# The output product of the last pair of tiles as seven half-size products, with operand sums on VectorE and weight sums made in slices ahead of it

## The chip, the core and the metric

The kernel runs on one core of one Trainium2 chip. The core has a matrix engine (TensorE: PE for its matmuls, PEld for its weight loads), VectorE (DVE), ScalarE (ACT), GpSimd (POOL) and SyncE (SP), which issues all of the kernel's transfers into one queue served by 16 DMA engines. The metric is the device time of one execution, in microseconds. Before the change the median of 3 runs is 935.18 us (934.85 to 935.95).

## What is computed

Attention in chunks of 64 tokens, and then a gated feed-forward layer with a root-mean-square norm, all in float32. There are 8 x 576 = 4608 tokens, 8 heads of 64, a model width of 512 and a hidden width of 1536.

```python
scores = scale * np.matmul(q_c, k_c.transpose(0, 1, 2, 4, 3))     # chunks of 64
scores = scores - np.max(scores, axis=-1, keepdims=True)
attn = np.exp(scores)
attn = attn / (np.sum(attn, axis=-1, keepdims=True) + 1e-09)
x = np.matmul(attn, v_c)                    # gathered to 4608 x 512
xn = x / np.sqrt(np.mean(x * x, axis=-1, keepdims=True) + 1e-06) * rms_g
g = xn @ w_gate                             # 512 x 1536
silu = g * (1.0 / (1.0 + np.exp(-g)))
out = (silu * (xn @ w_val)) @ w_out         # 1536 x 512
```

## The kernel before

**Tiles.** The 4608 tokens are nine tiles of 512. The first three ("plain", line 834) go one by one; the other six go as three pairs (line 909). A matmul takes 128 x 128 stationary and 128 x 512 moving values. Every float32 operand is split into a high part, rounded to the type that TensorE multiplies (F32R), and a low part, the rest; a product is three matmuls: high x high, high x low, low x high.

**A plain tile.** For each of 12 blocks f of 128 hidden columns, `gated` makes the gate and the value (24 matmuls), ACT and DVE make the gated result and its two parts, and `down` adds its share of the output to four PSUM banks (12 matmuls). During the first plain tile the weights are converted from 64-bit words; during the first two they are stored to DRAM in the form that the pairs read: `wsd` holds the operands of the up products, `wod` those of the output product (`wod[i]` for the f blocks 2i and 2i+1: both parts, 512 output columns).

**A pair, up.** For each of six f pairs i, `up_pair` (line 649) multiplies a 2 x 2 block matrix of weights by a 2 x 2 block matrix of two tiles of normed tokens with seven products instead of eight, named P1 to P7, in the order P1, P5, P6, P2, P3, P7, P4. One product is 12 matmuls (two outputs m, two halves of the contraction, three parts). It adds into a bank named a, b, c or d. After each one, `after` takes what it needs from PSUM: ACT copies or SiLU, DVE sums, POOL sums and the multiplications of gate by value. The results are `g`, six tiles, each of 2 f blocks x 2 token tiles x 512. The token operands `xp` are made by `x_sides` (line 590), with a scratch tile `t1` (one buffer); the weight operands are loaded by `ring_load` (line 626), three loads ahead (`AHEAD_R`).

**A pair, output.** For each of the two token tiles and each f pair, `split_g` (line 735) makes the two parts of g (ACT cast, DVE subtraction; two buffers of each), and `down` adds to four banks, 12 matmuls for each of 24 splits. The weights come from `wod` by `out_load`, three loads ahead, 1 MB each. At the end of a tile, four banks are copied out, alternately by DVE and ACT, and stored.

**Attention for the next pair.** While pairs one and two run, four units of 256 tokens each are made for the pair that follows. A unit is seven steps: load q, k and v; scores and softmax; a turn of the weights, written to DRAM (`away_e`); the turned weights read back (`eT`); the values (`ps_o`, matmuls); the same turn for its rows of x (`away_x`, back into `x` or `x2`). A counter is advanced once after each of the 42 up products and once in each of the 24 stretches of the output product; unit n has its seven steps at 4 + 10n + (-4, 0, 3, 5, 8, 11, 13). The third pair has no units.

**What sets the order.** From the second plain tile on PE's instructions run in the order in which the program writes them. The other engines' and SP's orders come from a planner that simulates the program with its own costs: an instruction is placed when its data and its buffer are there in that simulation, by its place in the program; those written inside `urgent()` count as 300 places earlier. Once placed, each queue keeps its order on the chip, and an instruction that has to wait holds those behind it.

## Time and profile before

| | us |
|---|---|
| median of 3 runs | 935.18 |
| range of the runs | 934.85 to 935.95 |
| the profiled execution | 936.39 |
| its span, first to last instruction | 934.6 |
| pair one, up products (368.0 to 492.5) | 124.5 |
| pair one, output product (492.5 to 559.6) | 67.1 |
| pair two, up products (559.6 to 684.1) | 124.5 |
| pair two, output product (684.1 to 751.2) | 67.1 |
| pair three, up products (751.19 to 865.43) | 114.24 |
| pair three, output product (865.43 to 930.72) | 65.29 |
| after the last matmul | 3.88 |

The stages before 368 us are the three plain tiles. The stage boundaries are read from the chain of waits, where PE goes from one product's name to the other. A row of a group gives the line, the engine, the operation, output<-inputs by the program's names, the count, then busy time and the mean duration in ns, then the idle time before it and what ended it. A row of the timeline begins with its start and its length in us. The granted clock of TensorE is 1.000 throughout.

### The profile page before, as it was taken

To read this page: it belongs to the slowest core of one execution; us is meant where nothing else is said; L and a number is where in the kernel's file an instruction comes from. 1 tells how busy PE (TensorE), PEld (TensorE's weight loads), DVE (VectorE), ACT (ScalarE), POOL (GpSimd) and SP (SyncE) were. 2 spreads that over 40 slices of the span, in tenths; PEclk is the share of its full clock that TensorE was granted. 3 is DMA by queue.
4 is the path that set the end of the run, shared out by engine and by line. 5 is a ranking of instruction groups with operands and counts; after the bars stand their busy time and mean duration, and the time that the engine had idled before them with its cause. 6 is when DMAs were issued, how large, how long until landed. Compare 5 with 4: busy or idle time off the path is not lost.

```text
span 934.6 us, 17360 instructions
## 1 busy us (share of the span) xinstructions
PE 905.9 (97%) x6936; PEld 742.2 (79%) x6936; DVE 516.2 (55%) x889; ACT 431.5 (46%) x697; POOL 172.7 (18%) x157
## 2 busy tenths in 40 slices
PE   4599999999999999999999999999999999999998
PEld 3478788888888788888888888888888888888886
DVE  5899983554546555754664735546656332333232
ACT  4999963453446543553444425445444223222222
POOL 0100012224200000233332002322330023224100
PEclk9999999999999999999999999999999999999999
DMA  8688998868975644767789666586987585337511
GB/s 338 248 310 309 329 367 318 264 236 250 308 275 150 187 148 154 270 218 280 253 288 348 269 269 256 213 289 188 335 311 265 239 329 211 135 135 296 243 46 46
DMA packets 78737, 231.84 MB, mean 248 GB/s; under 512 B 8384, under 2 KB 40128, under 8 KB 62912
## 3 DMA queue, kind: packets, MB, share of 16 engines
q1 hardware_dynamic: 78656, 230.72, 69.0%
q8 instruction: 55, 0.90, 0.4%
q14 instruction: 26, 0.21, 0.1%
HBM read 171.97 MB, written 58.72 MB: 247 GB/s over the span
## 4 chain that ended last, share of the span: by engine, by line
PE 85%; ACT 7%; DVE 4%; DMA 2%; issue 1%; SPq 1%; POOL 0%; ACTq 0%; DVEq 0%; POOLq 0%
PE acc L506 29%; PE ps_b L637 11%; PE ps_c L637 11%; PE ps_a L637 11%; PE ps_g L471 7%; PE ps_v L471 7%; PE ps_d L637 5%; PE ps_o L356 2%; PE ps_s L239 2%; ACT w L152 1%; ACT e L275 1%; ACT raw L153 1%; ACT parts L177 1%; DVE parts L185 1%; DMA x<-kT_dram 1%
## 5 line engine op out<-in xcount | busy, mean ns | idle before, releaser
L506 PE MATMUL acc<-wo,gh 128*128 128x512 f32 x576 | 177.6, 390 | 0.0
L506 PEld LDWEIGHTS acc<-wo,gh 128*128 128x128 f32 x576 | 108.0, 188 | 22.5
L506 PE MATMUL acc<-wo,gl 128*128 128x512 f32 x288 | 112.3, 390 | 0.0
L740 DVE TENSOR_TENSOR gl<-g,gh 128x512 fp32r<-128x512 f32 x72 | 49.7, 691 | 101.2 <-ACT gh L739 99.2
L637 PE MATMUL ps_b<-xp,wr 128*128 128x512 f32 x432 | 104.7, 391 | 0.0
L637 PE MATMUL ps_c<-xp,wr 128*128 128x512 f32 x432 | 104.3, 390 | 0.0
L637 PE MATMUL ps_a<-xp,wr 128*128 128x512 f32 x432 | 103.5, 390 | 0.0
L471 PE MATMUL ps_g<-xh,parts 128*128 128x512 f32 x288 | 97.1, 396 | 1.9 <-ACT sg L489 1.4
L739 ACT CAST gh<-g 128x512 fp32r<-128x512 f32 x72 | 44.8, 623 | 116.1 <-PE acc L506 110.9
L471 PE MATMUL ps_v<-xh,parts 128*128 128x512 f32 x288 | 95.7, 392 | 0.0
L637 PEld LDWEIGHTS ps_a<-xp,wr 128*128 128x128 f32 x432 | 80.9, 188 | 16.9
L637 PEld LDWEIGHTS ps_b<-xp,wr 128*128 128x128 f32 x432 | 80.6, 188 | 17.1
L637 PEld LDWEIGHTS ps_c<-xp,wr 128*128 128x128 f32 x432 | 80.8, 188 | 16.9
L506 PE MATMUL acc<-parts,gh 128*128 128x512 f32 x288 | 90.2, 394 | 0.0
L711 POOL TENSOR_TENSOR g<-u,u 128x512 f32<-128x512 f32 x18 | 23.2, 1289 | 342.1 <-DVE u L707 244.4
L423 POOL TENSOR_TENSOR ri<-ss,mhalf 128x1 f32<-128x1 f32 x36 | 23.7, 665 | 245.1 <-DVE ss L421 244.8
L471 PEld LDWEIGHTS ps_g<-xh,parts 128*128 128x128 f32 x288 | 54.3, 189 | 14.3 <-ACT sg L489 1.8
L471 PEld LDWEIGHTS ps_v<-xh,parts 128*128 128x128 f32 x288 | 54.5, 189 | 11.3
L506 PEld LDWEIGHTS acc<-wo,gl 128*128 128x128 f32 x288 | 54.1, 188 | 11.8 <-DVE gl L740 0.5
L506 PEld LDWEIGHTS acc<-parts,gh 128*128 128x128 f32 x288 | 53.3, 188 | 11.2
L506 PE MATMUL acc<-parts,gl 128*128 128x512 f32 x144 | 56.5, 392 | 0.0
L471 PE MATMUL ps_g<-xl,parts 128*128 128x512 f32 x144 | 56.4, 391 | 0.0
(105 smaller groups left out, 1393.2 us busy)
## 6 DMA issues: line engine op xcount, KB each, us to landing
wr<-wsd SPq DMA_DIRECT2D x63, 1024.0 KB, 7.8
wo<-wod SPq DMA_DIRECT2D x36, 1024.0 KB, 8.2
raw<-w_up_dram SPq DMA_DIRECT2D x12, 1024.0 KB, 9.4
vt<-v_dram SPq DMA_DIRECT2D x18, 512.0 KB, 6.7
wsd<-parts SPq DMA_DIRECT2D x18, 512.0 KB, 6.6
out_dram<-o SPq DMA_DIRECT2D x36, 256.0 KB, 2.2
qt<-qT_dram SPq DMA_DIRECT2D x17, 512.0 KB, 5.5
kt<-kT_dram SPq DMA_DIRECT2D x17, 512.0 KB, 5.9
```

The source lines that it names most:

```text
L152: nc.scalar.activation(w, high.bitcast(F32), AF.Abs, scale=2.0**16)
L153: nc.scalar.mul(low, low.bitcast(U32), 2.0**-29)
L177: nc.scalar.copy(parts[:, 0].rearrange("p i c -> p (i c)"), w)
L239: nc.tensor.matmul(st["s"][j][c * CH : (c + 1) * CH, pr], st["q"][rows, pr, tok : tok + CH], st["k"][rows, pr, tok : tok + CH], start=True ...
L356: nc.tensor.matmul(st["o"][(2 * c + t) * Q : (2 * c + t + 1) * Q, h * D : (h + 1) * D], eT[c][rows, t, h], vt[rows, c, h], start=True, sto ...
L423: nc.gpsimd.tensor_tensor(ri, ss, mhalf, op=ALU.pow)
L471: nc.tensor.matmul(ps, a[f][:, cols], b[dt], start=(dt == 0 and i == 0), stop=(dt == NDT - 1 and i == 2),)
L506: nc.tensor.matmul(acc[s], a[:, cols], b, start=(f == 0 and i == 0), stop=(f == NF - 1 and i == 2),)
L637: nc.tensor.matmul(ps, w[:, a, m, cols], xp[:, b, kt], start=start and kt == 0 and i == 0, stop=stop and kt == 1 and i == 2, skip_group_ch ...
L711: nc.gpsimd.tensor_tensor(g[:, 0, 1], kp["u2"], kept[0]["u2"], op=mult)
L739: nc.scalar.copy(gh, src)
L740: nc.vector.tensor_tensor(gl, src, gh.bitcast(F32), op=ALU.subtract)
```

## The change

In the last pair the output product is no longer two tiles one after the other. `last_down` treats it as a 2 x 2 block product: the stationary side is an f pair's weights (two f blocks by two halves of 256 output columns), the moving side the two f blocks by the two token tiles of g. It uses the same seven products and the same order as the up products, for each product all six f pairs, n = 0 to 41. One n is a split of one 128 x 512 operand and 6 matmuls (two blocks m of 128 output columns, three parts). The output comes out turned, 128 output columns by 512 tokens; it is stored so, and the host turns those 1024 rows.

- `last_sums` makes two differences of g's quarters after each up step i on DVE, into spare rows of `x` and `x2`, which no unit needs in the last pair. `split_next` updates the operand after its split in P5 and P2, on DVE.
- `split_g` gets a second pair of buffers in turn (those of the attention weights, `e` and `eT`), and the splits are asked for two ahead (`AHEAD_G`).
- `last_after` takes each product from PSUM and stores four quarters of 2 x 256 KB: after P2, P3, P7 and P4.
- The weights' sums are made in pairs one and two, by twelve slices of `out_sides`, six in each: steps 7n + 0 to 5 of the counter load a slice, copy three unsummed operands in DRAM, make five sums on DVE, round on ACT, subtract on DVE, store. The slice's tile has the tag of `t1` and its one buffer. `x_sides` takes `t1` at its first use instead of at its start. The result is a new DRAM tensor `wol`, read by `last_load`, four operands (1 MB) at a time.

```diff
+AHEAD_G = 2
+SIDE_STEPS = 0, 1, 2, 3, 4, 5
+NOS = (7 * NPR + 3) // 4
+INTO = {P1: "a", P2: "a", P6: "b", P7: "b", P5: "c", P3: "c", P4: "d"}
+FROM = {p: INTO[p] for p in (P1, P6, P5, P4)}
+LAST = P2, P7, P3, P4
...
+    wol_ = dram.tile([P, 7 * NPR, 2 * KH], F32, name="wol")
+    def out_sides(i, c):
+        at = {}
+        parts = wod[i].rearrange("p (a n c) -> p a n c", a=2, c=KH)[:, :, :, c * P : (c + 1) * P]
+        slots = wol_.rearrange("p (k i) c -> p i k c", i=NPR)[:, i, :, c * KH : (c + 1) * KH]
+        def load():
+            w = at["w"] = st.tile([P, 4, 2, P], F32, tag="t1", bufs=1, name="w")
+            for a in range(2):
+                nc.sync.dma_start(w[:, :, a], parts[:, a])
+        def plain():
+            for p, n in (P1, 0), (P2, 2), (P4, 3):
+                nc.sync.dma_start(slots[:, p].rearrange("p (a c) -> p a c", a=2), parts[:, :, n])
+        def sums():
+            w = at["w"]
+            nc.vector.tensor_tensor(w[:, :, 0], w[:, :, 0], w[:, :, 1], op=ALU.add)
+            a11, a21, a12, a22 = (w[:, n, 0] for n in range(4))
+            s1, s2, s4, s3 = (w[:, n, 1] for n in range(4))
+            for o, one, two, op in (
+                (s1, a21, a22, ALU.add),
+                (s2, s1, a11, ALU.subtract),
+                (s4, a12, s2, ALU.subtract),
+                (s3, a11, a21, ALU.subtract),
+            ):
+                nc.vector.tensor_tensor(o, one, two, op=op)
+        def high():
+            w = at["w"]
+            nc.scalar.copy(w[:, :, 0].bitcast(F32R), w[:, :, 1])
+        def low():
+            w = at["w"]
+            nc.vector.tensor_tensor(w[:, :, 1].bitcast(F32R), w[:, :, 1], w[:, :, 0], op=ALU.subtract)
+        def store():
+            w = at["w"].rearrange("p n a c -> p n (a c)")
+            nc.sync.dma_start(slots[:, P5 : P6 + 1], w[:, :2])
+            nc.sync.dma_start(slots[:, P3 : P7 + 1], w[:, 2:])
+        return [load, plain, sums, high, low, store]
...
-    def split_g(src):
-        gh = gp.tile([P, TT], F32R, name="gh")
-        gl = gp.tile([P, TT], F32R, name="gl")
+    def split_g(src, other=False):
+        pool, names = (att, ("e", "eT")) if other else (gp, ("gh", "gl"))
+        gh, gl = (pool.tile([P, TT], F32R, tag=n, name=n) for n in names)
...
+    def last_load(n):
+        k = min(4, 7 * NPR - 4 * n)
+        t = big([P, 4, 2, 2, P], F32R, "wo")
+        nc.sync.dma_start(
+            t[:, :k].rearrange("p n m a c -> p n (m a c)").bitcast(F32), wol_[:, 4 * n : 4 * n + k]
+        )
+        return t
+    def spare(i):
+        return (x, x2)[i // NSUB][:, i % NSUB]
+    def last_sums(i, g):
+        for o, one, two in (spare(i), g[:, 0, 1], g[:, 0, 0]), (g[:, 0, 1], g[:, 1, 1], g[:, 0, 1]):
+            nc.vector.tensor_tensor(o, one, two, op=ALU.subtract)
+    def last_down(t, gs, wos):
+        rows = out[t * TT : (t + 2) * TT, :].rearrange("(d a) c -> d (a c)", a=2)
+        split = {}
+        def split_next(n):
+            if n >= 7 * NPR:
+                return
+            p, i = divmod(n, NPR)
+            g, t1 = gs[i], spare(i)
+            src = {
+                P1: g[:, 0, 0], P5: t1, P6: t1, P2: g[:, 1, 0], P3: g[:, 1, 1], P7: g[:, 0, 1], P4: g[:, 1, 0]
+            }[p]
+            split[n] = split_g(src, n % 4 > 1)
+            with urgent():
+                if p == P5:
+                    nc.vector.tensor_tensor(t1, g[:, 1, 1], t1, op=ALU.subtract)
+                elif p == P2:
+                    nc.vector.tensor_tensor(g[:, 1, 0], t1, g[:, 1, 0], op=ALU.subtract)
...
+        for n in range(AHEAD_G):
+            split_next(n)
+        for n in range(7 * NPR):
+            p, i = divmod(n, NPR)
+            for k in range(n // 4, min(n // 4 + AHEAD_O, NOS)):
+                if k not in wos:
+                    wos[k] = last_load(k)
+            w = wos[n // 4][:, n % 4]
+            parts = split.pop(n)
+            for m in range(2):
+                if i == 0 and p in FROM:
+                    ps[m][FROM[p]] = bank(ps_h if p == P1 else ps_acc, f"ps_{FROM[p]}")
+                for k, (a, c) in enumerate(((0, 0), (0, 1), (1, 0))):
+                    nc.tensor.matmul(ps[m][INTO[p]], w[:, m, a], parts[c], ...)
+            split_next(n + AHEAD_G)
+            if i == NPR - 1:
+                with urgent():
+                    for m in range(2):
+                        last_after(p, m, ps[m], kept[m], store)
+    def last_after(p, m, b, kp, store):
+        # P1, P5: ACT copies; P6: one DVE sum; P2: ACT copy, store
+        # P3: one DVE sum, store; P7: two DVE sums, store
...
+        elif p == P4:
+            nc.vector.tensor_tensor(kp["p1"], kp["p1"], b["d"], op=ALU.subtract)
+            store(m, 1, 0, kp["p1"])
...
+        last_pair = b == NB - 1
+        if not last_pair:
+            for n in range(NPR):
+                for k, f in enumerate(out_sides(b * NPR // 2 + n // 2, n % 2)):
+                    at.setdefault(7 * n + SIDE_STEPS[k], []).append(f)
         for i in range(NPR):
-            gs.append(up_pair(i, step, wos))
+            gs.append(up_pair(i, step, wos, last_load if last_pair else out_load))
+            if last_pair:
+                last_sums(i, gs[i])
+        if last_pair:
+            last_down(t, gs, wos)
+            break
```

More of the change, by code (lines that the diff above doesn't have):

```diff
@@ L485, in gated @@
         sg = tmp_tile("sg")
-        gh = gp.tile([P, TT], F32R, name="gh")
-        gl = gp.tile([P, TT], F32R, name="gl")
+        gh = gp.tile([P, TT], F32R, tag="gh", name="gh")
+        gl = gp.tile([P, TT], F32R, tag="gl", name="gl")
         with urgent():
@@ L593, in x_sides, with t1 @@
         b11, b21, b12, b22 = x1[:, :, :2], x1[:, :, 2:], x2[:, :, :2], x2[:, :, 2:]
-        t1 = st.tile([P, 8, 2, 2 * Q], F32, tag="t1", bufs=1, name="t1")
         sub = ALU.subtract
+        later = {}
+        def t1():
+            if not later:
+                later[0] = st.tile([P, 8, 2, 2 * Q], F32, tag="t1", bufs=1, name="t1")
+            return later[0]
         def scale(x, dts):
@@ L611, in x_sides @@
             lambda: scale(x2, (0, 1)),
-            lambda: less(t1, b12, b11),
-            lambda: x_side(P5, t1),
+            lambda: less(t1(), b12, b11),
+            lambda: x_side(P5, t1()),
             lambda: scale(x2, (2, 3)),
-            lambda: less(t1, b22, t1),
-            lambda: x_side(P6, t1),
+            lambda: less(t1(), b22, t1()),
+            lambda: x_side(P6, t1()),
             lambda: x_side(P3, b22),
@@ L619, in x_sides @@
             lambda: x_side(P7, b12),
-            lambda: less(b21, t1, b21),
+            lambda: less(b21, t1(), b21),
             lambda: x_side(P4, b21),
@@ L647, in hold, with up_pair @@
         return xs.tile([P, TT], F32, tag="xs", name=name)
-    def up_pair(i, step, wos):
+    def up_pair(i, step, wos, wo_load):
         g = big([P, 2, 2, TT], F32, "g")
@@ new lines, in last_down, with store @@
+    def last_down(t, gs, wos):
[15 more added lines that the diff above has]
+                    nc.vector.tensor_tensor(g[:, 1, 0], t1, g[:, 1, 0], op=ALU.subtract)
+        def store(m, half, h, o):
+            at = half * KH + m * P
+            nc.sync.dma_start(rows[at : at + P, h * TT : (h + 1) * TT], o)
+        ps, kept = [{}, {}], [{}, {}]
+        for n in range(AHEAD_G):
[11 more added lines that the diff above has]
+                for k, (a, c) in enumerate(((0, 0), (0, 1), (1, 0))):
+                    nc.tensor.matmul(
+                        ps[m][INTO[p]],
+                        w[:, m, a],
+                        parts[c],
+                        start=p in FROM and i == 0 and k == 0,
+                        stop=p in LAST and i == NPR - 1 and k == 2,
+                        skip_group_check=True,
+                    )
+            split_next(n + AHEAD_G)
[3 more added lines that the diff above has]
+                        last_after(p, m, ps[m], kept[m], store)
@@ new lines, in last_after @@
+    def last_after(p, m, b, kp, store):
+        if p == P1:
+            kp["p1"] = hold("p1")
+            nc.scalar.copy(kp["p1"], b["a"])
+        elif p == P5:
+            kp["p5"] = hold("p5")
+            nc.scalar.copy(kp["p5"], b["c"])
+        elif p == P6:
+            kp["u2"] = hold("u2")
+            nc.vector.tensor_tensor(kp["u2"], b["b"], kp["p1"], op=ALU.add)
+        elif p == P2:
+            c11 = hold("c11")
+            nc.scalar.copy(c11, b["a"])
+            store(m, 0, 0, c11)
+        elif p == P3:
+            nc.vector.tensor_tensor(kp["u2"], b["c"], kp["u2"], op=ALU.add)
+            store(m, 0, 1, kp["u2"])
+        elif p == P7:
+            nc.vector.tensor_tensor(kp["p1"], b["b"], kp["p1"], op=ALU.add)
+            nc.vector.tensor_tensor(kp["p5"], kp["p1"], kp["p5"], op=ALU.add)
+            store(m, 1, 1, kp["p5"])
+        elif p == P4:
+            nc.vector.tensor_tensor(kp["p1"], kp["p1"], b["d"], op=ALU.subtract)
+            store(m, 1, 0, kp["p1"])
@@ L1003 @@
     rows = res.results[0]["out_dram"]
+    last = N - 2 * TT
+    rows = np.concatenate([rows[:last], rows[last:].reshape(DM, 2 * TT).T])
     turned = rows[2 * TT :].reshape(-1, 4, 2, Q, DM).transpose(0, 2, 1, 3, 4).reshape(-1, DM)
```

9 lines of the change are left out of this document (3 added, 6 removed).

## The prediction, made before the changed kernel was run

> **What bounds the kernel now.** I read the share of each engine first, then the busy time stage by stage, then the end of the chain of waits, and last the queues that feed it.
>
> ```profile
> PE 905.9 (97%) x6936; PEld 742.2 (79%) x6936; DVE 516.2 (55%) x889; ACT 431.5 (46%) x697; POOL 172.7 (18%) x157
> 276.70:368.00 91.30, 90.02 (x1054) 73.44 (x1053) 49.38 (x101) 44.81 (x65) 4.33 (x8) 1.00 0.52 154
> 368.00:492.50 124.50, 124.50 (x1146) 102.12 (x1145) 78.93 (x147) 61.55 (x93) 39.65 (x35) 1.00 0.75 263
> 559.60:684.10 124.50, 124.50 (x1146) 102.13 (x1145) 70.17 (x139) 57.97 (x89) 39.69 (x35) 1.00 0.73 257
> 751.19:865.43 114.24, 114.24 (x505) 94.63 (x505) 38.04 (x56) 30.55 (x51) 36.76 (x29) 1.00 0.60 228
> 865.43:930.72 65.29, 65.28 (x288) 53.73 (x287) 18.55 (x27) 15.48 (x26) 2.05 (x2) 1.00 0.25 100
> ```
>
> The five stretches are: most of the third plain tile; the up products of pairs one and two; the up products and the output product of the last pair. After the stretch and its length come the busy times of PE, PEld, DVE, ACT and POOL with their counts, the granted clock, the DMA share and GB/s. PE is full in each of the last four. So a matmul removed there is worth its spacing, and every stall newly put there is paid.
>
> ```profile
> 862.71 2.72 PE ps_d L637 x12
> 865.43 65.29 PE acc L506 x288
> 930.72 0.02 issue
> 930.75 0.58 ACT o L730
> ```
>
> The chain ends in the output product itself: 288 matmuls in 65.29 us, 226.7 ns each, without a break. An up product has the same spacing, 2.72/12 = 226.7 ns, with the weights as the stationary side, as they are in the new product. What follows the last matmul is one copy and its store.
>
> **Part 1, the output product.** It becomes 7 products x 6 pairs of f x 2 halves x 3 parts = 252 matmuls of the same shape. 36 fewer x 0.2267 = **8.16 us** less; the stage would take 57.13.
>
> [...]
>
> **Part 2, what feeds it.** A split now serves 6 matmuls, 1.36 us, where it served 12.
>
> ```profile
> L740 DVE TENSOR_TENSOR gl<-g,gh 128x512 fp32r<-128x512 f32 x22 | 15.2, 692 | 43.4 <-ACT gh L739 41.4 <-PE acc L506 2.0
> L739 ACT CAST gh<-g 128x512 fp32r<-128x512 f32 x22 | 13.7, 624 | 44.4 <-PE acc L506 44.4
> ```
>
> ACT has 0.62 us of work per 1.36, DVE 0.69; where P5 and P2 also update an operand, DVE has 1.38 per 1.36. Twelve such steps lose 12 x 0.02 = 0.2 us at worst and nothing if the splits run ahead. Four pairs of buffers let them: a split waits only for the product four before it. Today ACT waits for PE 44.4 us in this stage because two pairs are all it has. The evacuations add 10 DVE and 6 ACT operations in all, spread between products: DVE 42 + 12 + 10 = 64 x 0.69 = 44 of 57 us. Taken as 0; if splits did not overlap, see the third rival.
>
> The operand sums (12 DVE operations, 8.3 us) fall into the last pair's up stage, where DVE is busy 38 of 114 us. Only the sums of the last f pair come late:
>
> ```profile
> 864.89 1.30 POOL L705 TENSOR_TENSOR g<-p,p 128x512 f32<-128x512 f32 x1
> 866.37 1.29 POOL L717 TENSOR_TENSOR g<-p,p 128x512 f32<-128x512 f32 x1 [0.18 <-DVE p L713]
> 843.70 22.56 SPq L745 DMA_DIRECT2D wo<-wod  x12
> ```
>
> One waits on DVE for POOL until 866.2, with the next splits queued behind it; the first four splits have nothing to wait for and cover 5.4 us of PE. Uncovered it would be 866.2 + 0.7 - 865.4 = 1.5 us. Taken as 0. The weights come as 11 transfers instead of 12 and, as the last row shows, are issued before the stage begins: 0.
>
> **Part 3, the end.** The last operation is a DVE subtraction (0.69) where it was an ACT copy (0.58), then a store of the same 256 KB: **+0.11 us**.
>
> **Part 4, the slices.** Each of twelve slices is seven transfers (two loads of 256 KB, three copies of 128 KB from DRAM to DRAM, two stores of 256 KB), five DVE sums, one ACT cast and one DVE subtraction. The nearest rows:
>
> ```profile
> L305 DVE TENSOR_TENSOR e<-ps_s,mx 128x256 f32<-128x256 f32 x16 | 5.9, 412 | 0.0
> L574 DVE TENSOR_TENSOR w<-w,side 128x512 fp32r<-128x512 f32 x24 | 17.7, 771 | 17.1 <-ACT side L572 17.0
> L572 ACT CAST side<-w 128x512 fp32r<-128x512 f32 x24 | 13.6, 618 | 1.6 <-DVE gl L498 1.6
> q1 hardware_dynamic: 78656, 230.72, 69.0%
> w<-wfd SPq DMA_DIRECT2D x12, 512.0 KB, 5.4
> wsd<-w SPq DMA_DIRECT2D x24, 256.0 KB, 3.5
> ```
>
> DVE: 0.69 + 4 x 0.41 + 0.77 = 3.10 us a slice, 18.6 a pair: pair one's up stage goes from 78.9 to 97.5 of 124.5 us, pair two's to 88.8. ACT gains 3.7 a pair. Both fit. DMA: 1408 KB a slice, 17.3 MB in all; 230.72 MB takes 69.0% of the span, so this takes 5.2%, 48 us of all sixteen queues, into two stages that have 124.5 x (0.25 + 0.27) = 65 us free. It fits, narrowly. SP: 7 issues x 0.43 = 3.0 us a slice. A store waits on SP for DVE's subtraction, and the next load for that store (3.5 us, against two products, 5.44, between them); the ring loads queued behind are three ahead of PE, 3 x 5.44 = 16 us, and cover such waits.
>
> Where it can reach PE is the chain of the attention units, whose matmuls stand at fixed places in PE's order:
>
> ```profile
> 450.25 4.23 SPq L330 DMA_DIRECT2D away_e<-e  x2
> 454.54 0.42 SPq L629 DMA_DIRECT2D wr<-wsd  x1
> ...
> L339 SPq DMA_DIRECT2D eT<-away_e x8: 303/407/428, 455.1 to 460.0; - x8
> DMA to landing us min/median/max: 2.2/4.7/5.3
> 464.98 1.48 PE L356 MATMUL ps_o<-vt,eT 64*32 64x64 f32 x128
> PE ps_o L356 <- DMA eT<-away_e: 1.3, 2, 1.1
> ```
>
> In pair one's third unit the last read back is issued at 460.0 and lands 2.2 to 5.3 us later; PE uses it at 465.0. The margin is 2.8 us at best and none at worst. In the third plain tile (last row) PE already waited 1.3 us for such a read. A slice's load (512 KB, 5.4 us) written between a unit's write and its read back (the first and third units of a pair have one) holds SP and the queues ahead of the reads.
>
> The planner need not keep these places:
>
> ```profile
> 261.85 0.33 SPq L629 DMA_DIRECT2D wr<-wsd  x1
> 320.94 2.95 PE ps_g L471 x12
> ```
>
> A ring load written behind the product at 320.9 was issued at 261.8, because its buffer and data were there. The copies need no buffer, and the slices only one, so they may run far ahead, into the third plain tile, where DMA is 52% busy. That tile and the pairs have the same tight spot. Bounds of the cost: a gain of 1.3 us if a new order happens to take the existing wait away; nothing, if every slice falls into free time; and 2 x 5.4 us = 10.8 if each pair's third unit loses a whole load. I take one more wait of the size of the one on record, **+1.3 us**, since the spare DMA time is larger than the added work.
>
> **Sum.** The profiled execution took 936.39 us, 1.79 around its span of 934.6; the runs' median is 935.18, 1.21 lower. -8.16 + 0.11 + 1.3 = -6.75: a profiled execution of 929.6, a median of **928.4 us**.
>
> **Rivals.**
>
> *All of it hidden.* For it: DVE, ACT, DMA and SP have room in every stage. Against: the read back without margin. 935.18 - 8.05 = 927.1 us.
>
> *The attention units give half back.* For it: the rows of the third unit. Against: the slices' transfers can be issued in SP's idle stretches. Two to four units late by 1.3 to 2.6 us, in the middle 3 x 1.7 = 5.1: 932.2 us.
>
> *The splits set the pace, and the product does not get shorter.* If ACT's cast, DVE's subtraction and DVE's update follow each other without overlap, P5 and P2 take 0.62 + 0.69 + 0.69 = 2.0 us a step, 0.64 above PE's, and the other thirty 1.31, no loss: 12 x 0.64 = 7.7 us of the gain gone, 934.8 us. Against it: ACT and DVE are separate queues with four buffer pairs.
>
> *DVE is held by a slice's load (slower).* The sums are written two products after the load, 5.44 us. DVE takes its work in order, so a late load holds the evacuations behind it.
>
> ```profile
> 380.29 0.69 DVE L707 TENSOR_TENSOR u<-ps_c,u 128x512 f32<-128x512 f32 x1 [0.50 <-PE ps_c L637]
> wr<-wsd SPq DMA_DIRECT2D x63, 1024.0 KB, 7.8
> DMA to landing us min/median/max: 5.0/8.0/13.4
> ```
>
> The tightest of these is the one shown (L707): it must free its bank within half a product and one more, 4.08 us, so DVE may be held 4.08 - 0.69 = 3.4 us before PE stalls. A slice is then harmless up to a landing of 5.44 + 3.39 = 8.83 us and costs the excess beyond. Twelve slices cost more than the 8.05 us gained, and 1.87 for 0.2%, from a mean landing of 8.83 + 9.92/12 = 9.7 us. For it: ring loads in pair one land after 5.0 to 13.4 us (last row), and more transfers will queue. Against: 512 KB take 5.4, and the planner may place the sums later. At 10 us: 12 x 1.17 = 14.0, so 927.1 + 14.0 = 941.1 us.
>
> [...]
>
> **How the numbers follow.** About 0.2% (1.87 us) is what a measurement of this kernel can tell from no change: faster is below 933.3, slower above 937.05. Forecast 0.38, all hidden 0.20, attention half back 0.18 (of it 0.02 above 933.3), splits 0.08 (same), DVE held 0.16 (slower). Faster 0.38 + 0.20 + 0.16 = 0.74, same 0.10, slower 0.16. The range: below all hidden by half a microsecond, for a part of the 1.3 us wait gone, to just above the splits rival: 926.6 to 935.4, leaving out the slow case and little else.
>
> **What would show it.** Right: 252 matmuls at 226.7 ns without a gap in the last stage, about 57.1 us; DVE near 44 us there; the last store after a DVE subtraction. Part 4 wrong for the worse: PE idle before L356 on eT, or before a product on DVE's L707 or L713, with DVE waiting for a slice's load; a mean landing above 9 us. Better: PE full in both up stages, 124.5 us each. The forecast falls if the last stage takes over 60 us, or if the stages ahead of it grow by more than 3.

## The result, and the profile after

The median of four runs is 944.96 us (941.53 to 946.50), against 935.01 for the kernel before on the same chip (934.59 to 935.95). The ratio is 1.0096, with a 95% interval of 1.0078 to 1.0115: about 1% slower. The profiled execution is the shortest of the four, 941.53 us with a span of 939.4, so the stages below explain 4.8 us of the 10. The other executions have no trace.

The busy shares and the transfers' rows (KB each, median us to landing):

```profile
PE 902.5 (96%) x6900; PEld 736.6 (78%) x6900; DVE 576.7 (61%) x1009; ACT 451.5 (48%) x729; POOL 173.3 (18%) x157
q1 hardware_dynamic: 107504, 246.46, 74.6%
w<-wod SPq DMA_DIRECT2D x24, 256.0 KB, 5.8
wol<-w SPq DMA_DIRECT2D x24, 256.0 KB, 2.9
```

PE has 36 matmuls fewer. The queue's share is 5.6 points up, where 5.2 were forecast; in time of all sixteen queues that is 0.746 x 939.4 - 0.690 x 934.6 = 56 us for the 48 of the prediction. The stages, with the columns of the prediction's first fence:

```profile
276.70:367.40 90.70, 89.45 (x1048) 72.80 (x1047) 48.63 (x100) 44.44 (x65) 4.33 (x8) 1.00 0.64 190
367.40:499.29 131.89, 126.23 (x1145) 102.15 (x1145) 92.48 (x183) 64.81 (x99) 39.70 (x35) 1.00 0.85 288
499.29:567.74 68.45, 67.18 (x417) 55.22 (x417) 36.26 (x49) 24.80 (x39) 3.15 (x4) 1.00 0.81 306
567.74:697.18 129.44, 125.97 (x1145) 102.10 (x1144) 86.36 (x175) 61.69 (x95) 41.12 (x36) 1.00 0.84 287
697.18:764.37 67.19, 67.19 (x417) 55.54 (x418) 34.98 (x46) 24.70 (x38) 2.26 (x3) 1.00 0.72 278
764.37:878.61 114.24, 114.24 (x505) 94.59 (x505) 45.08 (x69) 31.39 (x52) 35.13 (x28) 1.00 0.60 229
878.61:935.75 57.14, 57.12 (x252) 46.95 (x251) 40.60 (x62) 27.63 (x46) 3.55 (x3) 1.00 0.23 93
```

The last stage gives what it was to give: 65.29 to 57.14. The up stages of pairs one and two, where the slices stand, grow by 7.39 and 4.94, pair one's output product by 1.36. Together with the 8.15 of the last stage, 0.6 us less ahead of pair one and 0.2 less at the end, that is the span's 4.8. PE, full in both up stages before, now idles. Its waits in pair one's up stage (total, times, longest):

```profile
PE ps_c L696 <- DMA wr<-wsd: 2.8, 2, 2.2
PE ps_b L696 <- DMA wr<-wsd: 2.1, 2, 1.1
PE ps_o L363 <- DMA eT<-away_e: 0.7, 1, 0.7
```

It waits mostly for its own weights, the ring loads, and only 0.7 us for the attention unit that the prediction watched. In pair two's up stage it waits 1.2 us for attention units, 1.1 for ring loads and 1.1 for the first weights of the output product. What VectorE and SP wait for in pair one's up stage (the last two fields are again times and longest; the rows of the slices and the read back, others left out):

```profile
DVE w L550 <- DMA w<-wod: 9.1, 4, 4.4
...
SPq L542 <- DMA wol<-w: 10.9, 3, 7.4
SPq L346 <- DMA away_e<-e: 10.0, 4, 2.8
SPq L571 <- DVE w L567: 8.7, 2, 8.5
```

A slice's load (L542) waits on SP until the store of the slice before it has left the one buffer, and a store (L571) waits for VectorE. Ring loads stand behind such waits on SP's queue. The chain of waits passes through such a place (start, length):

```profile
470.70 11.89 DMA wol<-w
...
483.75 9.68 DMA wr<-wsd
...
493.57 3.00 PE ps_b L696 x12
```

A slice's store lands after 11.89 us; the next slice's load waits for that, and the ring load behind it on SP is issued at 483.75 and lands just before PE resumes.

How much delay a ring load can bear is its lead, the time from its issue to PE's first use of it, less its landing time. It shows at a load that the prediction has among its rows, the one issued in the kernel before at 454.54, behind an attention unit's write that held SP for 4.23 us. It lands after 5.5 us, and PE first uses it here:

```profile
462.17 2.88 PE L637 MATMUL ps_c<-xp,wr 128*128 128x512 f32 x12
```

That is a lead of 7.6 us with 2.1 to spare, though the load is three ahead in the program. In the kernel after the same load is issued at 459.81, lands after 5.2 us, and PE waits:

```profile
465.14 2.98 PE L696 MATMUL ps_c<-xp,wr 128*128 128x512 f32 x12 [2.15 <-DMA wr<-wsd]
```

This load is late because it was issued 5.3 us later; the one at 483.75 is issued 7.1 us later than in the kernel before (476.68) and lands after 9.7 us in place of 6.2. In the third pair, without attention units, the shortest lead of the kernel before is 19 us.

Two windows of 20 us, first of the kernel before and then of after, show how uneven the 0.75 and 0.85 of the stage are:

```profile
400.00:420.00 20.00, 20.00 (x269) 16.29 (x268) 13.05 (x27) 10.54 (x18) 7.52 (x7) 1.00 0.58 210
460.00:480.00 20.00, 20.00 (x269) 16.29 (x268) 11.33 (x24) 9.25 (x17) 7.39 (x7) 1.00 0.82 301
```

```profile
400.00:420.00 20.00, 20.00 (x268) 16.29 (x268) 12.85 (x28) 9.18 (x16) 7.52 (x7) 1.00 0.91 301
460.00:480.00 20.00, 17.10 (x252) 13.42 (x251) 10.92 (x23) 7.45 (x14) 7.40 (x7) 1.00 0.97 321
```

The second is nearly full, and there PE loses 2.9 of 20 us. A high share alone does not do it: at 0.91, in the first, PE loses nothing.

### The profile page after: what moved, and what is told of

Read it like the earlier page. It is cut to its first block, busy times and chain, and to the rows that moved or that the text cites. A ratio compares the mean times of both kernels' runs of the same rounds, so it can differ in the third digit from the quotient of the medians.

```text
span 939.4 us, 17558 instructions
## 1 busy us (share of the span) xinstructions
PE 902.5 (96%) x6900; PEld 736.6 (78%) x6900; DVE 576.7 (61%) x1009; ACT 451.5 (48%) x729; POOL 173.3 (18%) x157
## 4 chain that ended last, share of the span: by engine, by line
PE 74%; DMA 11%; ACT 7%; DVE 4%; SPq 2%; issue 1%; POOL 0%; DVEq 0%; ACTq 0%; POOLq 0%
PE acc L513 22%; PE ps_c L696 8%; PE ps_a L696 8%; PE ps_b L696 8%; PE ps_g L478 7%; PE ps_v L478 7%; PE ps_d L696 4%; DMA wr<-wsd 3%; PE ps_b L864 2%; PE ps_c L864 2%; PE ps_a L864 2%; DMA w<-wod 2%; DMA wol<-w 2%; PE ps_o L363 2%; DMA eT<-away_e 1%
## 5 line engine op out<-in xcount | busy, mean ns | idle before, releaser
L513 PE MATMUL acc<-wo,gh 128*128 128x512 f32 x384 | 118.7, 390 | 2.3 <-ACT xu L385 1.3
L513 PEld LDWEIGHTS acc<-wo,gh 128*128 128x128 f32 x384 | 71.8, 188 | 18.1 <-ACT xu L385 1.7
L798 ACT CAST gh<-g 128x512 fp32r<-128x512 f32 x64 | 39.9, 623 | 87.8 <-PE acc L513 73.5
L799 DVE TENSOR_TENSOR gl<-g,gh 128x512 fp32r<-128x512 f32 x64 | 45.1, 708 | 58.4 <-ACT gh L798 58.3
L513 PE MATMUL acc<-wo,gl 128*128 128x512 f32 x192 | 74.7, 389 | 0.0
L500 DVE TENSOR_TENSOR sg<-ps_v,sg 128x512 f32<-128x512 f32 x36 | 24.8, 690 | 54.2 <-PE ps_v L478 45.6
```

The lines of the kernel that those rows point to most:

```text
L500: nc.vector.tensor_tensor(sg, pv, sg, op=ALU.mult)
L513: nc.tensor.matmul(acc[s], a[:, cols], b, start=(f == 0 and i == 0), stop=(f == NF - 1 and i == 2),)
L798: nc.scalar.copy(gh, src)
L799: nc.vector.tensor_tensor(gl, src, gh.bitcast(F32), op=ALU.subtract)
```

## The experiments

| kernel | median us | ratio to before, 95% | start of pair one | pair one | pair two | third up |
|---|---|---|---|---|---|---|
| before | 935.01 | | 368.0 | 191.6 | 191.6 | 114.2 |
| after | 944.96 | 1.0096 (1.0078 to 1.0115) | 367.4 | 200.3 | 196.6 | 114.2 |
| 1 no slices | 926.98 | 0.9905 (0.9886 to 0.9925) | 367.7 | 191.8 | 191.6 | 114.2 |
| 2 transfers only | 939.51 | 1.0039 (1.0019 to 1.0059) | 368.6 | 199.5 | 194.6 | 114.2 |
| 3 sums only | 929.28 | 0.9933 (0.9914 to 0.9952) | 365.8 | 193.6 | 191.6 | 114.2 |
| 4 stores of g only | 934.06 | 0.9997 (0.9980 to 1.0015) | 366.7 | 194.5 | 195.6 | 114.2 |
| 5 copies only | 930.97 | 0.9957 (0.9942 to 0.9972) | 371.4 | 191.5 | 191.5 | 114.2 |
| 6 after without copies | 940.72 | 1.0060 (1.0037 to 1.0083) | 366.8 | 201.6 | 195.4 | 114.2 |
| 7 sums on POOL | 939.81 | 1.0050 (1.0031 to 1.0070) | 370.2 | 196.4 | 193.6 | 114.2 |
| 8 two buffers | 945.31 | 1.0122 (1.0084 to 1.0159) | 373.0 | 204.2 | 198.0 | 114.2 |
| 9 every 11th step | 944.01 | 1.0093 (1.0076 to 1.0110) | 370.7 | 199.4 | 197.5 | 114.2 |
| 10 in the plain tile, POOL | 952.66 | 1.0186 (1.0169 to 1.0203) | 392.8 | 191.5 | 191.5 | 114.2 |
| 11 in the plain tile, DVE | 946.83 | 1.0125 (1.0110 to 1.0141) | 386.0 | 191.5 | 191.5 | 114.2 |
| 12 issued by POOL | 1037.84 | 1.1109 (1.1087 to 1.1131) | | | | 114.2 |
| 13 issued by ACT | 995.86 | 1.0653 (1.0623 to 1.0682) | | | | 114.2 |
| 14 in the third pair | 936.74 | 1.0009 (0.9998 to 1.0019) | 370.3 | 191.5 | 191.5 | 121.0 |
| 15 the same, no copies | 927.87 | 0.9923 (0.9901 to 0.9944) | 366.8 | 191.5 | 191.5 | 114.6 |

The last four columns are of one profiled execution each (run 8's is the longest of its four), "pair" being up and output stage together. A ratio is to runs of the kernel before beside that run on the same chip; their medians lie between 935.01 and 935.98.

**1. No slices.** The last product reads the plain weights where their sums should stand.

```diff
-            t[:, :k].rearrange("p n m a c -> p n (m a c)").bitcast(F32), wol_[:, 4 * n : 4 * n + k]
+            t[:, :k].rearrange("p n m a c -> p (n m a c)").bitcast(F32), wod[n % NPR][:, : k * DM]
...
-        if not last_pair:
+        if False:
...
```

> The changed kernel without its twelve slices: no loads, copies, sums or stores, and the last pair's weights are read from the plain operands in DRAM (the same eleven transfers, but the wrong operands: the last pair's output leaves out the weights' sums). Theory that the whole loss comes from the slices and the last stage gives its full gain: 935.0 - 8.05 = 927 us, within 0.7. Rival, that something else of the change (the operand sums on DVE, the splits, the operand differences) also costs: above 929 us.

926.98 us. Its stages from pair one on:

```profile
367.69:559.44 191.75, 191.75 (x1562) 157.37 (x1561) 114.26 (x194) 86.33 (x131) 42.82 (x38) 1.00 0.75 275
559.44:751.07 191.63, 191.63 (x1562) 157.37 (x1561) 105.49 (x186) 82.63 (x127) 42.83 (x38) 1.00 0.71 259
751.07:865.31 114.24, 114.24 (x505) 94.63 (x505) 45.10 (x69) 31.41 (x52) 35.15 (x28) 1.00 0.59 228
865.31:922.40 57.09, 57.09 (x252) 46.96 (x251) 40.55 (x62) 27.62 (x46) 3.54 (x3) 1.00 0.23 94
```

PE is full throughout. The new product with its splits, operand sums and evacuations is worth its whole 8 us, and the slices cost 944.96 - 926.98 = 18.0. The next runs take that apart.

**2. The slices' transfers alone**, so that `wol` holds no sums.

```diff
-        return [load, plain, sums, high, low, store]
+        return [load, plain, None, None, None, store]
...
```

> The changed kernel with the slices' transfers alone: load, copies and store stay, the five sums, the rounding and the subtraction are left out (the operands stored for P5, P6, P3 and P7 are unsummed, so the last pair's output leaves out the weights' sums). Theory S, that transfers and SP's order cost the time: 940 to 947 us. Theory D, that DVE held by a load costs it: 927 to 930 us, since no DVE instruction is left that waits for a load.

939.51 us: 12.5 more than without slices, just below the range of theory S; theory D falls. SP and the queue in pair one, from the chain of waits (short rows of issue left out):

```profile
450.01 8.55 DMA wol<-w
...
458.58 0.39 SPq L542
...
459.02 7.22 DMA w<-wod
...
466.26 0.30 SPq L346
...
468.99 11.77 DMA wr<-wsd
```

Store, next load and the attention's read back (L346) follow each other on SP, and the ring load behind them goes out at 468.99 and takes 11.77 us.

**3. The sums alone**: each tile is filled on chip by ACT in place of the loads, there are no copies and no stores, and the last product reads as in run 1.

```diff
-                nc.sync.dma_start(w[:, :, a], parts[:, a])
+            nc.scalar.copy(
+                w.rearrange("p n a c -> p (n a) c"),
+                ident.rearrange("p (o c) -> p o c", o=1).broadcast_to([P, 8, P]),
+            )
...
-        return [load, plain, sums, high, low, store]
+        return [load, None, sums, high, low, None]
...
```

> The changed kernel with the slices' compute alone: five DVE sums, the ACT rounding and the DVE subtraction stay, on a tile that ACT fills from the identity (1 us more on ACT a slice); no load, copy or store, and the last pair reads the plain operands (its output leaves out the weights' sums). Theory S: 927 to 928.5 us. A theory that the added DVE work itself delays the evacuations, whatever the load does: 933 us or more. DVE held by a load (theory D) cannot show here, so it too gives 927 to 928.5.

929.28 us: 2.3 more than without slices, though the intervals of the two ratios overlap; by the trace the two pairs are 1.8 us longer. PE waits once for VectorE:

```profile
PE ps_d L698 <- DVE u L767: 1.3, 1, 1.3
```

**4. As many bytes, in plain stores.** No slices; in each of the first two pairs g, complete when it is stored, goes to a scratch tensor, 12 stores of 512 KB, 6 MB a pair, as many bytes as a pair's slice loads and stores.

```diff
+                for h, run in enumerate((P, KH)):
+                    scr = scratch[h].rearrange("n p c -> n p c")
+                    nc.sync.dma_start(scr, gs[i][:, h].rearrange("p t (n c) -> p (t n) c", c=run))
...
```

> No slices; in pairs one and two each of the six gated tiles g is also stored once to a scratch tensor, 1 MB in two stores (runs of 512 and 1024 bytes), 6 MB a pair, as many bytes as six slices' loads and stores. No buffer and no DVE instruction waits for them, and SP finds them ready. The last pair reads the plain operands (its output leaves out the weights' sums). Theory B: 934 to 940 us, most of the 12.5 us that transfers alone cost over 927. Theory H: 926 to 930 us.

934.06 us, 7.1 more than without slices. No operation of an engine is added. But SP does not find the stores ready, as was expected: in pair one it waits 38.5 us for POOL's products ahead of them (20.5 in five waits, 18.0 in three), where without slices it waits elsewhere. So this is the price of the bytes, of their issue and of these waits together. At the ring load looked at above it is not the issue: that comes at 453.83, 0.7 us sooner than in the kernel before, but the load lands after 8.1 us in place of 5.5:

```profile
462.02 2.98 PE L696 MATMUL ps_c<-xp,wr 128*128 128x512 f32 x12 [1.06 <-DMA wr<-wsd]
```

The two pairs as a whole:

```profile
366.68:561.13 194.45, 192.18 (x1562) 157.13 (x1561) 112.41 (x194) 86.28 (x131) 42.92 (x38) 1.00 0.85 301
561.13:756.69 195.56, 192.38 (x1562) 157.20 (x1561) 105.40 (x186) 82.50 (x127) 42.87 (x38) 1.00 0.81 288
```

The shares, 0.85 and 0.81, are near those of after's up and output stages (0.85 and 0.81, 0.84 and 0.72).

**5. The copies alone**, the last product as in run 1.

```diff
-        return [load, plain, sums, high, low, store]
+        return [None, plain, None, None, None, None]
...
```

> Of the slices only the transfers from DRAM to DRAM that copy the plain halves of the weights remain; slices are not loaded, summed or stored, and the last product reads the plain halves where the sums should stand, so its output leaves the weights' sums out. Bytes-everywhere theory: the copies (36 of 128 KB, ahead of the pairs for the most part) ran in the attention of the first three tiles, where the DMA share is 0.64, and cost nothing there: 926.5 to 928. If the copies delay the attention units, 929 to 932; if the 18 us hang on them, 938 or more.

930.97 us: 4.0 more than without slices, though the planner had moved all copies ahead of pair one (issued from 185.7 to 334.2 us). Pairs one and two are undisturbed; pair one starts 3.7 us later. In the third plain tile:

```profile
280.00:320.00 40.00, 38.35 (x519) 30.92 (x518) 20.88 (x48) 22.28 (x31) 2.16 (x4) 0.96 0.85 245
```

Without copies that window has a share of 0.59 and a granted clock of 1.00. If the whole window lengthened in proportion to the clock, 0.96 would be worth 0.04 x 40 = 1.6 us, an estimate; the matmuls' times there were not taken apart. Of the 3.7, 1.4 us are not the copies': PE's first `ps_o` product starts at 13.88 us here and at 12.46 in run 1, long before the first copy is issued. That leaves 2.3 us for the copies in this execution. In the profiled execution of after, with its copies in the same places (183.6 to 329.1), pair one starts at 367.4, no later than in run 1, and the clock is 1.000: the copies do not cost the same in every execution.

**6. After without the copies.** The last product's loads fetch the plain halves from `wod`, 18 transfers of 256 KB, and `wol` keeps only the sums.

```diff
-        return [load, plain, sums, high, low, store]
+        return [load, None, sums, high, low, store]
...
+            if p in PLAIN_AT:
+                nc.sync.dma_start(
+                    t[:, j].rearrange("p a m c -> p a (m c)").bitcast(F32),
+                    wod[i].rearrange("p (a n c) -> p a n c", a=2, c=KH)[:, :, PLAIN_AT[p]],
+                )
...
```

> The kernel after with its slices in the first two pairs as they were, and only the copies from DRAM to DRAM taken away (the last product's loads fetch the plain halves from where they stand). The result is complete. If the copies' 4 us of the run with copies alone add to the rest: 940 to 942, with pair one starting where it does in after and the gain in the up stages. If the copies ran in room that is free, as their place ahead of the pairs says: 943.5 to 946.

940.72 us, 4.2 below after. The sum of the stages of pairs one and two in the two profiled executions is the same, 396.98 and 396.97 us; the medians differ, and the intervals of the ratios touch. So the gain is not in the up stages, where it was expected. That the copies cost their 4 us here too fits, and is not more than that.

**7. The sums on POOL.**

```diff
-            nc.vector.tensor_tensor(w[:, :, 0], w[:, :, 0], w[:, :, 1], op=ALU.add)
+            nc.gpsimd.tensor_tensor(w[:, :, 0], w[:, :, 0], w[:, :, 1], op=ALU.add)
...
-                nc.vector.tensor_tensor(o, one, two, op=op)
+                nc.gpsimd.tensor_tensor(o, one, two, op=op)
```

> The changed kernel with the five sums of a slice on POOL instead of DVE; everything else stays, and so does the result. Theory S: 942 to 947 us, the loads still hold SP and the queues. Theory D: DVE no longer waits for a load, 930 to 937 us; POOL waits in its place, with the sums of P7 behind it, which have 8 us of room.

939.81 us, 5.1 below after, between the ranges of the two theories: more than the sums cost alone. What else lies on VectorE's queue in after is its wait for a slice's load, 9.1 us in pair one, with PSUM evacuations behind it; on POOL the same wait holds only the gate's products.

**8. Two buffers**: every other slice uses two scratch tiles in place of `t1`, so that a load need not wait for the store before it.

```diff
+            if c:
+                at["a"], at["s"] = (tmp_tile("w").rearrange("p (n c) -> p n c", c=P) for _ in range(2))
```

> The changed kernel with a second buffer for the slices: every other slice takes two tiles of the pool of temporaries instead of the tile it shares with t1 (and its four results leave in four stores a slice instead of two). Bytes and sums are the same. Theory H, that SP is held by a slice's load that waits for the store before it (17.2 us in three waits in pair one of the run with transfers alone): 931 to 937 us. Theory B, that the added bytes keep the queues full and every transfer late: 942 to 947 us.

945.31 us, no change (the profiled execution took 952.02). The wait of a slice's load for a store is gone from SP, and PE still waits for ring loads (pair one):

```profile
PE ps_c L699 <- DMA wr<-wsd: 4.4, 2, 3.6
```

So the one buffer was not what made the weights late, and theory H falls. That SP is held by a slice at all is not ruled out by it: the slices' stores still wait there for ACT and VectorE, 14 us in pair one's up stage.

**9. Slices every eleventh step** in place of every seventh, reaching into the output stage.

```diff
-                    at.setdefault(7 * n + SIDE_STEPS[k], []).append(f)
+                    at.setdefault(11 * n + SIDE_STEPS[k], []).append(f)
```

> The slices of after, in the same two pairs, one every eleventh step of the pair's counter in place of every seventh, so that they reach into the output stage. The result is complete. If the cost is set by the bytes that a pair carries in all, it stays at 943 to 946. If it is set by how closely the slices stand in the up stage (the DMA share of 0.84 there), the up stages of pairs one and two fall by some third of their 7.4 and 4.9 us, the output stages grow by less, and the time is 938 to 942.

944.01 us, no change: spreading the slices over more of the pair does not help.

**10 and 11. Slices in the third plain tile**, out of operands still on chip, sums on POOL and on VectorE, each slice stored when ready. It needs no loads.

```diff
-        parts = wod[i].rearrange("p (a n c) -> p a n c", a=2, c=KH)[:, :, :, c * P : (c + 1) * P]
+        parts = out_parts[i].bitcast(F32).rearrange("p a b (h c) -> p a (b h) c", c=KH)
...
+            for n in range(2 * NPR):
+                for f in out_sides(n // 2, n % 2, w2):
+                    at.setdefault(n, []).append(f)
...
```

> The twelve slices are made in the third plain tile, from the operands that are still in on-chip memory: no loads and no copies from DRAM to DRAM; POOL makes the five sums (it is busy 4 of 91 us there), ACT and DVE round and subtract, in two buffers in the space of x2, free until that tile's third unit. Stores: 896 KB a slice. The result is complete. By H and by B alike nothing is left in the pairs: 926 to 929 us. Rival: the third plain tile's attention units, where PE waited 1.3 us already, pay for it: 930 us or more.

> As the run with POOL's sums in the third plain tile, but with the sums on VectorE, 37 us of work beside 49 of 91. 927 to 930 us; if DVE work rather than waiting for data makes the evacuations late there, 931 us or more, and more than the run with POOL.

952.66 and 946.83 us, where 926 to 930 were expected; the rival came true, and VectorE's sums cost less than POOL's. The pairs are undisturbed (191.5 us), but pair one starts 25 and 18 us late. In run 10, up to its start:

```profile
PE ps_s L246 <- DMA kt<-kT_dram: 6.6, 1, 6.6
PE ps_o L363 <- DMA eT<-away_e: 5.7, 4, 4.6
PE ps_s L246 <- DVE gl L505: 3.4, 1, 3.4
```

The third plain tile has the attention chain without margin that the prediction described. With the slices beside it PE waits for that tile's loads, its read backs and VectorE; which of the slices' operations or stores does it was not taken apart.

**12 and 13. The slices' transfers issued by POOL, and by ACT**, in place of SP; the first of four such lines, which in run 13 has `nc.scalar`:

```diff
-                nc.sync.dma_start(w[:, :, a], parts[:, a])
+                nc.gpsimd.dma_start(w[:, :, a], parts[:, a])
```

> The kernel after with all transfers of the slices (loads, copies, stores) issued from POOL in place of SP; the bytes, the sums and the places are the same, the result is complete. Theory Q (SP's order: ring loads and the attention units' reads stand behind the slices' waits and issues on SP): the 14 us that pairs one and two lost shrink by half or more, 932 to 938, unless POOL, held by the same waits, makes its gate multiplications late. Theory B (bytes: whatever queue issues them, the ring loads land late beside them): 940 to 946. If POOL's waits reach PE through its sums (P7, P3, P4): over 946, with PE or PEld waits on POOL or on VectorE behind it.

> The same with the slices' transfers issued from ACT. Theory Q: 932 to 938, unless ACT, held by the wait for the buffer or for VectorE's subtraction, evacuates PSUM late. Theory B: 940 to 946. If ACT's waits reach PE: over 946, with PE waiting on ACT copies or casts.

1037.84 and 995.86 us, far worse. An engine that computes now carries the waits of the transfers. Run 12, PE's largest wait and the wait behind it, and then run 13's:

```profile
PE ps_d L696 <- DVE u L765: 31.8, 3, 11.9
...
DVE w L550 <- DMA w<-wod: 106.4, 10, 14.8
```

```profile
PE ps_d L696 <- DVE u L765: 16.3, 3, 7.6
...
DVE w L550 <- DMA w<-wod: 52.5, 8, 10.7
```

The loads go out late: they stand in order behind the engine's other work and the slices' other waits (POOL in run 12: 57.4 us for VectorE's subtractions ahead of the stores, 24.8 for a store to free the buffer). VectorE, in order, waits 106.4 and 52.5 us for them, and PE for VectorE. This is the rival "VectorE is held by a slice's load" in full size. The runs therefore don't tell SP's order from the bytes, as they were to. These two moved both of a slice's directions off SP, to engines that PE's work waits for, and took 1.11 and 1.07 times as long as before.

**14. All twelve slices in the third pair's up stage**, one every three steps, two buffers (`t1` and rows of x2 that are free by then).

```diff
+            if c:
+                w = x2[:, 2:].rearrange("p s c -> p (s c)").rearrange("p (n a c) -> p n a c", n=4, a=2)
...
-        if not last_pair:
+        if last_pair:
...
-                    at.setdefault(7 * n + SIDE_STEPS[k], []).append(f)
+                    at.setdefault(3 * n + SIDE_STEPS[k], []).append(f)
```

> All twelve slices are made in the up stage of the third pair, one every third counter step, from the same loads, sums on VectorE and stores; two tiles take turns for them (the one of after, and one in rows of the input that no longer serve there). The result is complete. Theory T: what costs the 18 us of after is that the slices' transfers and their sums share the first two pairs with the attention units, where the DMA share goes to 0.8 to 1.0. In the third pair there is no attention unit, VectorE works 45 of its 114 us and the DMA share is 0.60. Pairs one and two then take their 191.7 us of the kernel without slices, the third up stage grows by 0 to 4 us over 114.2, and the time is 928 to 931 us. Rival R: the slices' bytes cost the same wherever they are put, since ring loads land late beside any of them: third stage grows by 12 us or more, time over 938. Rival S: the last product waits for the last slices' stores and for the copies of their sums behind them: PE idle at the head of the last stage, 932 to 937.

936.74 us. Both pairs are full again, the third up stage grows from 114.2 to 121.0, pair one starts 2.6 us late as in run 5. In the third stage:

```profile
PE ps_d L700 <- DVE u L769: 4.0, 2, 2.8
...
DVE w L554 <- DMA w<-wod: 11.4, 3, 6.4
DVE x L554 <- DMA x<-wod: 8.0, 3, 4.6
```

No wait of PE for a ring load is left, and none at the head of the last stage; PE waits for VectorE, which waits for slices' loads. So T is right on the pairs and its third stage 3 us too short; R's mechanism is not there; the time lies in the range of S by luck, since the wait of S is not there. What T had missed, as far as the waits show, is a load and its sum too close in program order, and the delay ahead of pair one.

**15. The same with three buffers** (`t1`, `x2[:, 2:]`, `x2[:, :2]`), four steps from a load to its first sum, a store two steps after the subtraction, and no copies, as in run 6 (the lines are against run 14).

```diff
-SIDE_STEPS = 0, 1, 2, 3, 4, 5
+SIDE_STEPS = 0, 0, 4, 5, 6, 8
...
+            k = (2 * i + c) % 3
...
-        return [load, plain, sums, high, low, store]
+        return [load, None, sums, high, low, store]
...
-                    at.setdefault(3 * n + SIDE_STEPS[k], []).append(f)
+                    at.setdefault((33 if n == 11 else 8 * n // 3) + SIDE_STEPS[k], []).append(f)
```

> The slices stay in the third pair, with three buffers in place of two, four counter steps in place of two between a slice's load and its first sum, and the store two steps after the last operation on VectorE. The copies of the plain halves from DRAM to DRAM are gone: the last product's loads fetch the plain halves from where they stand, in 18 transfers of 256 KB. The result is complete. Theory T (the first two pairs are left alone, the third has room if nothing on VectorE waits for a slice's load, and the copies cost the 4 us that they cost alone): pair one starts at 368, the third up stage lasts 114 to 116, the last stage 57.2, time 927 to 929.5. Rival R (bytes beside the ring loads cost PE time wherever they are): third up stage 119 or more, 932 to 934. Rival S (the last stage now waits for its 18 smaller loads): PE idle ahead of L881 on the loads, last stage 60 or more, 930 to 934.

927.87 us, ratio 0.9923 (0.9901 to 0.9944): faster than before and than after, and by the medians 0.9 us from the kernel that makes no sums at all. PE waits for nothing from pair one on. The third pair and the last stage:

```profile
749.88:864.48 114.60, 114.58 (x506) 94.52 (x505) 70.42 (x129) 36.53 (x62) 35.66 (x28) 1.00 0.88 312
864.48:921.60 57.12, 57.12 (x253) 46.95 (x251) 40.59 (x62) 27.58 (x46) 3.54 (x3) 1.00 0.29 108
```

The third stage carries the same slice loads, sums and stores as after's two pairs, at a share of 0.88, and costs 0.4 us. VectorE still waits 8.9 us for slice loads there, and has the time. Ring loads land after up to 14.0 us in this stage, no sooner than in after's pair one (13.8), but the shortest lead is 10.2 us, and that load lands after 7.8.

## Why the prediction was wrong, point by point

**Part 1 held.** 252 matmuls in 57.14 us, forecast 57.13, 226.7 ns each.

**Part 2 held.** From pair three's start on PE waits for nothing; VectorE is busy 40.6 us in the last stage where 44 were counted (62 operations of 0.65 us for 64 of 0.69). The rival in which the splits set the pace is out.

**Part 3** gave +0.11; the end became 0.2 us shorter. It doesn't matter.

The forecast with everything hidden, 927.1, is what run 1 measured, 926.98: without Part 4 the sum was right. (Beside run 1 the kernel before took 935.98, so the gain is 8.0 to 9.0, with an interval of 1.8 to either side.)

**Part 4 failed.** Its term was +1.3 us; it measured 18.0 (944.96 - 926.98). By the stages of the profiled executions pairs one and two carry 13.6 of it; the rest has no trace. Two sentences of the prediction carried the term.

The step that failed is "the ring loads queued behind are three ahead of PE, 3 x 5.44 = 16 us, and cover such waits". Three ahead is the place in the program, not the time on the chip: SP issues these loads behind the attention units' transfers, and in the kernel before the lead was already down to 7.6 us with 2.1 to spare. PE waited 4.9 us for ring loads in pair one's up stage, the largest part of its waits there. The kernel before already showed it, in the load at 454.54 and the product at 462.17.

"It fits, narrowly": 48 us of queue time into 65 us free. That time was 56 us, and the use of a stage's mean was not right either. In run 4 the ring load that had 2.1 us to spare landed 2.6 us later (8.1 for 5.5), at a mean share of 0.85 over its pair.

The parts by difference of medians: copies 4.0 (run 5), the stores of as many bytes 7.1 (run 4), what the slices' transfers cost beyond these 12.5 - 4.0 - 7.1 = 1.4, sums 2.3 (run 3), in all 14.8. The other 3.2 appear only when sums and transfers come together; run 7, which takes VectorE out of the wait for loads, gives 5.1 back. Three limits of this account. The parts are of different runs, each good to about 2 us (the intervals reach 0.0015 to 0.0023 to either side). By the stages the split comes out otherwise: the pairs are 10.7 us longer in run 2 than in run 1 and 6.7 in run 4, so the slices' order and waits on SP would be 4.0, while ahead of pair one run 2 is 0.9 us late and not 4.0. And how much of the whole is SP's issue order and how much queue time stays open: single loads show both (459.81 in after is issued late, 453.83 in run 4 lands late, 483.75 in after does both), and runs 12 and 13 changed too much.

The bounds were wrong for the same reason. The upper one, 10.8, priced only the attention units, which lost 0.7 us in pair one and 1.2 in pair two.

**The rivals.** "Attention units give half back" named the wrong reader in the main: in the two up stages PE waited 6.0 us for ring loads and 1.9 for read backs. "VectorE is held by a slice's load" had the sign, and its place shows in after (VectorE waits 9.1 us for loads, the weight loads of a product behind L765 1.5), but not its condition: the halves of slice loads landed after a median of 5.8 us, well below the 9.7 from which it was to decide. It explains at most the 3 to 5 us of run 7, and the largest waits of runs 12 and 13.

The mean of 771 ns that the prediction read at L574 comes from two of 24 operations (1714 and 1777 ns; the median is 684), both begun while one of POOL's sums ran. After's trace shows the same at a slice's subtraction, whose median is 692 ns:

```profile
648.22 1.29 POOL L759 TENSOR_TENSOR p<-p,p 128x512 f32<-128x512 f32 x1 [8.63 <-DVE p L758]
648.31 1.74 DVE L567 TENSOR_TENSOR w<-w 128x512 fp32r<-128x512 f32 x1
```

Seven of the slices' operations on VectorE are longer in this way, each while an operation of POOL ran, by about 6 us together: the two halves' sum takes up to 1.66 us for 0.69, the subtraction up to 1.74. That POOL's operation is the cause is not shown beyond this coincidence, and what it costs PE is open; with the sums on POOL the kernel was 5.1 us faster.

**What would show it.** Three of the signs came: stages ahead grown by more than 3 us, PE idle on eT, and VectorE's L765 (L707 of before) late with VectorE waiting for a slice's load. What cost most, PE idle on wr, was not on the list.

## What to carry to other kernels

Before work is put into a stage, look at the lead of each load of the critical engine there, from its issue to its first use, against its landing time; how many loads it is ahead in the program and the stage's mean share said little here: three loads ahead, at a mean share of 0.75, the shortest lead was 7.6 us where 16 were assumed.

Put background transfers into a stage where the leads are long, even if it is already busy: for the same loads, sums and stores the third pair, at a share of 0.88, paid 0.4 us (run 15 against run 1) and the two attention pairs 13.6 (run 6 against run 1). The place is not the whole of that difference: run 15 also has three buffers and a longer way from load to sum, and run 14, in the same place without them and with the copies, paid 6.8 us in that stage. The three buffers and the longer way were not tried in the attention pairs.

Give a load that an in-order engine consumes a distance in program order well beyond its landing time. In run 14 two steps of 2.72 us lay between them, the halves landed after 4.2 and 5.2 us in the median, and VectorE waited 19.4 us in six waits and PE 4.0 for VectorE; in run 15, with four steps and a third buffer, VectorE waited 8.9 and PE not at all. Fetch in a later load what would otherwise be copied in DRAM first: without the copies after was 4.2 us faster, and run 5 shows them costing 2.3 to 4.0.

## What the runs showed of the hardware

In some stretches in which PE idled the granted clock was lower. Run 10 shows it (the kernel before is at 1.000 throughout); the two longest waits in this window are 3.4 and 3.1 us:

```profile
280.00:320.00 40.00, 32.45 (x426) 26.16 (x427) 25.92 (x53) 22.81 (x33) 21.28 (x35) 0.91 0.77 231
```

The 40 us after it are at 0.91 too. They have the wait of 6.6 us, and the matmuls behind that wait took longer:

```profile
335.57 1.99 PE ps_s L246 x64
337.56 4.41 PE ps_g L478 x12
341.97 2.75 PE ps_v L478 x12
```

The same three without a wait ahead of them, in the kernel before:

```profile
319.85 1.09 PE ps_s L239 x64
320.94 2.95 PE ps_g L471 x12
323.89 2.72 PE ps_v L471 x12
```

So this stall of PE cost 2.4 us more than its length. In run 12, with waits of up to 11.9 us, the 40 slices of the page show the lower clock beside PE's busy tenths:

```profile
PE   5699899899999997666799966777999999999998
...
PEclk9999999999999998787899987897999999999999
```

Idle time alone does not give it. PE idles in the first slices of run 12 too, with the clock in the highest tenth, and in run 10 it idles 18.8 of the first 40 us at 1.00. The 40 us from 360 of run 11 are at 0.93 with 0.05 us of idle time, the 0.96 of run 5 goes with 1.65 us, and in run 1, without copies, the same window idled 1.82 us at 1.00. What lowers the clock is open.
